# A refitted static schedule for windowed attention followed by an MLP mixer: zero-stride score mask, later masks, a new DMA model in the planner

## The chip, the cores and the metric

The kernel runs on one core of one Trainium2 chip. The metric is the device time in microseconds (us), of which the median of several executions is quoted. A profile gives the span of one execution, which is about 1.8 us shorter than the time measured for it. The engines are called as in the profile: PE (TensorE, matmuls), PEld (TensorE weight loads), DVE (VectorE), ACT (ScalarE), POOL (GpSimd) and SP (SyncE, here only an issuer of transfers).

## The reference, cut to what matters

```python
# attention: q, k, v are (4, 8, 768, 64) fp32
scores = (1/sqrt(64)) * q @ k^T
keep   = (key < 4) | ((0 <= query - key) & (query - key < 128))   # 4 sink keys + a window of 128
a      = softmax(where(keep, scores, -1e9)); x = a @ v            # -> x: (4, 768, 512)
# mixer
h  = relu(x^T @ w_tok1) @ w_tok2        # over the sequence, 768 -> 256 -> 768
u  = x + h^T
out = u + relu(u @ w_ch1) @ w_ch2       # over the channels, 512 -> 1536 -> 512
```

Only the blocks of the scores near the diagonal and the four sink keys are computed. Heads go in eight groups of four (groups 0 and 1 are batch 0, groups 4 and 5 batch 2, and so on).

## The kernel before

Every piece of work is a task with a duration, engines that may run it, and a priority. A planner simulates the engines and the transfers while the kernel is built. The order in which tasks start in that simulation is the order in which they are written to each engine, and that order is then fixed. Priorities are built from the stage and a table of corrections, `BIAS`, that was fitted.

```python
LOADS = "v0 v1 tok1 tok2 ch1a ch1b ch1c ch2a ch2b q2 k2 v2 q3 k3 v3".split()   # POOL's load queue
DMA_LAG = 1.2
LATE_LAG = 4.0
LATE_AT = 57
BIAS = {'ca2': 15, 'ut3': -0.6, 'tok11': -0.3, 'ca2.1': -8, ...}

        def drain(to):                    # the planner's model of the DMA
            ...
                heads = [x for x in queues.values() if x and x[0][1] <= drained + 1e-9]
                ...
                    step = min([step] + [x[0][2] * len(heads) for x in heads])
                    for x in heads:
                        x[0][2] -= step / len(heads)          # queues share equally
                ...
                        finish(x.pop(0)[0], drained + (LATE_LAG if drained > LATE_AT else DMA_LAG if drained > 14 else 1.0))
```

The lag is the time that the planner allows between the end of a transfer's share and its semaphore. It is 1.0 us up to a planned time of 14 us, then 1.2 us, and 4 us after 57 us. The masks of the early groups are added on PE (an additive mask, `mneg`, times the identity); later groups are multiplied by `mask0` or `mask1` after the exponential.

```python
    mneg = sb.tile([P, 2, 2, 2, P], BF16, name="mneg")       # every block stored twice
    ...
                        for i in range(2):
                            nc.tensor.matmul(bank(slot)[:, i, 0:w], ident,
                                             mneg[:, min(u, 1)].rearrange("p x c q -> p (x c q)")[:, 0:w],
                                             start=True, stop=False, skip_group_check=True)
    ...
    t_mask = add("DVE", 0.5, lambda t: nc.vector.memset(mask0, 1.0), prio=1)
    t_mask = add("POOL", 0.8, lambda t: build_mask(mask0), [t_mask], prio=1.5)
    ...
```

The softmax here doesn't subtract the row's maximum and nothing guards it: scores larger than these inputs give would overflow.

## Time and profile before

The time before was 207.21 us (206.95 to 207.47, three runs).

| what | value | view |
|---|---|---|
| PE busy | 198.4 of 205.6 us, 97% | page, part 1 |
| granted PE clock | 9 tenths or more in every slice; mean 0.999 | page, part 2; list of cores |
| chain that ended last | 85% PE | page, part 4 |
| first transpose / first channel matmul / last matmul start | 6.06 / 30.54 / 202.13 us | trace |

The page of the kernel before, cut: part 1 (busy time, share of the span and instructions of each engine), the rows of PE and of its granted clock in forty slices of the span, and part 4 (the chain that ended last, by engine).

```profile
PE 198.4 (97%) x1633; PEld 115.4 (56%) x1633; DVE 97.1 (47%) x230; ACT 109.5 (53%) x184; POOL 72.9 (35%) x123
PE   7889999999989999999999999999999999999993
PEclk9999999999999999999999999999999999999999
PE 85%; DMA 9%; DVE 3%; issue 1%; POOL 0%; SPq 0%; POOLq 0%; DVEq 0%
```

PE is full except in the first 15 us (slices 1 to 3), in slice 12 (about 60 us) and in the last slice. A busy PE need not stream at its best: the Trainium skill, Perfetto Trace Analysis, section Identifying the Most-Contended Engine, says that the busy share of matmuls is a poor measure of how near one is to the limit. So I used start times. Successive 512-column matmuls start 216 ns apart when nothing stands in the way, and a distance clearly longer is a stall. The first 11 matmuls, which only warm the engine, were 427 ns apart. The Trainium skill, TensorE: Matmul & The Clock Gate, section "Wait — 56ns, not 53.3ns?", gives 215.7 ns for the warm array and 426.7 for the cold one; this trace agrees with both.

The waits of PE in the kernel before (what PE wrote, and its line; what it waited for; us in total, times, longest):

```profile
PE ps_ga L1038 <- DVE warm L340: 1.3, 1, 1.3
PE ps_gb L789 <- DVE x_bb L816: 0.9, 1, 0.9
PE ps_sa L696 <- ACT kTa L334: 0.7, 1, 0.7
PE ps_ga L640 <- DVE qbb L336: 0.6, 1, 0.6
PE ps_gd L794 <- DMA vaa<-in_v_dram: 0.3, 1, 0.3
PE ps_gc L794 <- DVE pTb L725: 0.2, 1, 0.2
```

The wait for `warm` is the start of the program. All the others together are 2.7 us, little more than 1% of the time. With the first 6 us and the tail left aside, that is the budget of a better order. The 0.9 us for `x_bb` are the one at 60 us:

```profile
61.05 0.27 PE L789 MATMUL ps_gb<-vsink,pka 128*128 128x260 bf16 x1 [0.86 <-DVE x_bb L816]
```

(The timeline gives the start, the duration, engine, line, operation, and in brackets the idle time before and what ended it.)

### The profile page before, as it was taken

Reading aid. Unit: us, or ns where it says so; the run is one execution under the profiler, and the core shown is the slowest. Engines: PE = TensorE matmul, PEld = TensorE weight load, DVE = VectorE, ACT = ScalarE, POOL = GpSimd, SP = SyncE. Lnnn points to the kernel's source line nnn. Section 1 sums busy time; section 2 is a strip of 40 time slices with the busy share of each in tenths; the row PEclk is TensorE's granted clock in tenths of the full one; section 3 lists DMA queues with packets and bytes.
Section 4 is the critical chain, followed back from the end, with each engine's and each line's share of the span. In section 5 each row is a group of like instructions: output and inputs, shape, how many; then the busy total and the mean of one; then the engine's idle time right before and its main releaser. Section 6 shows DMA issues by size and latency. Waiting matters only on the chain.

```text
span 205.6 us, 4197 instructions
## 1 busy us (share of the span) xinstructions
PE 198.4 (97%) x1633; PEld 115.4 (56%) x1633; DVE 97.1 (47%) x230; ACT 109.5 (53%) x184; POOL 72.9 (35%) x123
## 2 busy tenths in 40 slices
PE   7889999999989999999999999999999999999993
PEld 2436776565557566665565544575565445655453
DVE  7679470166969948403284333862365222001122
ACT  2799667788866872178721306948612204753200
POOL 8918981016006799302997100204840000000000
PEclk9999999999999999999999999999999999999999
DMA  5999999999499959999969968620012442001122
GB/s 180 364 199 186 205 197 203 340 272 167 142 300 205 217 80 147 150 153 237 222 162 146 195 149 172 211 45 3 0 51 75 98 137 102 3 0 51 51 105 102
DMA packets 74869, 30.97 MB, mean 151 GB/s; under 512 B 63650, under 2 KB 71202, under 8 KB 74850
## 3 DMA queue, kind: packets, MB, share of 16 engines
q0 software_dynamic: 29680, 10.22, 41.5%
q1 hardware_dynamic: 43938, 18.85, 41.2%
q10 hardware_dynamic: 1232, 1.64, 2.3%
q8 instruction: 13, 0.21, 0.4%
q14 instruction: 6, 0.05, 0.1%
HBM read 26.77 MB, written 6.29 MB: 161 GB/s over the span
## 4 chain that ended last, share of the span: by engine, by line
PE 85%; DMA 9%; DVE 3%; issue 1%; POOL 0%; SPq 0%; POOLq 0%; DVEq 0%
PE ps_gd L938 9%; PE ps_ga L957 8%; PE ps_gb L938 8%; PE ps_ga L938 8%; PE ps_gb L957 7%; DMA vaa<-in_v_dram 7%; PE ps_gc L957 7%; PE ps_gd L957 6%; PE ps_gc L938 6%; DMA k32a<-in_k_dram 3%; PE ps_sb L696 3%; PE ps_sa L696 2%; PE ps_gc L860 2%; PE ps_ga L860 1%; PE ps_gb L860 1%; DVE pTa L734 1%
## 5 line engine op out<-in xcount | busy, mean ns | idle before, releaser
L938 PEld LDWEIGHTS <-w_ch 128*128 128x128 bf16 x384 | 36.8, 98 | 25.7 <-issue 0.6
L957 PEld LDWEIGHTS <-v 128*128 128x128 bf16 x312 | 28.3, 98 | 28.1 <-issue 1.4
L957 PE MATMUL ps_ga<-w_ch,v 128*128 128x512 bf16 (+1 forms) x96 | 23.4, 366 | 0.0
L919 ACT ACTIVATE v<-ps_ga 128x384 bf16<-128x384 f32 x20 | 9.8, 491 | 23.8 <-PE ps_ga L938 18.9
L957 PE MATMUL ps_gd<-w_ch,v 128*128 128x512 bf16 x72 | 18.5, 379 | 0.0
L957 PE MATMUL ps_gb<-w_ch,v 128*128 128x512 bf16 (+1 forms) x72 | 16.6, 352 | 0.0
L919 ACT ACTIVATE v<-ps_gd 128x384 bf16<-128x384 f32 x25 | 12.3, 491 | 8.0 <-PE ps_gd L938 7.6
L957 PE MATMUL ps_gc<-w_ch,v 128*128 128x512 bf16 (+1 forms) x72 | 16.4, 352 | 0.0
L919 ACT ACTIVATE v<-ps_gb 128x384 bf16<-128x384 f32 x21 | 10.3, 491 | 7.6 <-PE ps_gb L938 7.4
L938 PE MATMUL ps_gd<-uTa,w_ch 128*128 128x384 bf16 x60 | 12.2, 326 | 0.0
L725 POOL TENSOR_TENSOR pTc<-pTc,mask 128x512 bf16<-128x512 bf16 x3 | 3.5, 1151 | 23.1 <-ACT pTc L714 23.1
L336 POOL CAST kbb<-k32b 128x768 bf16<-128x768 f32 x6 | 5.4, 920 | 17.2 <-DMA k32b<-in_k_dram 17.2
L938 PE MATMUL ps_ga<-uTb,w_ch 128*128 128x384 bf16 x56 | 11.4, 326 | 0.0
L938 PE MATMUL ps_gd<-uTb,w_ch 128*128 128x384 bf16 x56 | 11.4, 326 | 0.0
L938 PE MATMUL ps_gb<-uTa,w_ch 128*128 128x384 bf16 x52 | 10.6, 326 | 0.0
L860 PEld LDWEIGHTS <-w_tok 128*128 128x128 bf16 x96 | 9.0, 98 | 2.4 <-issue 0.4
L379 POOL DMA_DIRECT2D vaa<-in_v_dram x4 | 6.0, 1493 | 12.0 <-PE ps_gc L798 11.1
L714 ACT ACTIVATE pTa<-ps_sb 128x1024 bf16<-128x1024 f32 (+1 forms) x7 | 6.5, 929 | 6.2 <-PE ps_sb L696 6.2
L938 PE MATMUL ps_gb<-uTb,w_ch 128*128 128x384 bf16 x44 | 9.0, 326 | 0.0
L336 POOL CAST qbb<-q32b 128x768 bf16<-128x768 f32 x7 | 6.1, 884 | 6.3 <-DMA q32b<-in_q_dram 6.3
L938 PE MATMUL ps_ga<-uTa,w_ch 128*128 128x384 bf16 x40 | 8.1, 326 | 0.0
L919 ACT ACTIVATE v<-ps_gc 128x384 bf16<-128x384 f32 x13 | 6.4, 491 | 2.8 <-PE ps_gc L938 2.5
(318 smaller groups left out, 435.5 us busy)
## 6 DMA issues: line engine op xcount, KB each, us to landing
q32a<-in_q_dram SPq DMA_DIRECT2D x4, 384.0 KB, 4.2
vaa<-in_v_dram POOLq DMA_DIRECT2D x4, 384.0 KB, 11.6
vab<-in_v_dram POOLq DMA_DIRECT2D x4, 384.0 KB, 10.9
w_ch<-in_moe_w_ch_dram POOLq DMA_DIRECT2D x3, 512.0 KB, 7.7
w_ch<-in_moe_w_ch_dram POOLq DMA_DIRECT2D x2, 768.0 KB, 12.0
out_dram<-oa SPq DMA_DIRECT2D x6, 256.0 KB, 2.0
q32b<-in_q_dram SPq DMA_DIRECT2D x8, 192.0 KB, 4.8
k32b<-in_k_dram SPq DMA_DIRECT2D x8, 192.0 KB, 5.1
```

What stands on the lines that cost most here:

```text
L336: on(t).tensor_copy(out=o, in_=i)
L379: t = add(eng, hold, lambda t: e.dma_start(out=o, in_=i), deps, prio=prio, dma=work)
L696: nc.tensor.matmul(bank(slot)[:, i, at:at + w].rearrange("p (c q) -> p c q", q=P), qkT(kT, g, j)[ds(64 * i, 64), kt], qkT(qT, g, j)[ds(64 ...
L714: nc.scalar.activation(dst[:, :, 512 * u:512 * u + w], bank(slot)[:, :, 0:w], AF.Exp, scale=scale)
L725: on(t).tensor_tensor(out=dst[:, :, 0:2 * P], in0=dst[:, :, 0:2 * P], in1=mask0.rearrange("p i c q -> p i (c q)"), op=ALU.mult)
L734: nc.vector.tensor_tensor(out=v3, in0=v3, in1=mask1.rearrange("p o c q -> p o (c q)").to_broadcast([P, full - lo, 2 * P]), op=ALU.mult)
L860: nc.tensor.matmul(flat(slot)[:, 0:GH * D], w_tok1[:, n, ts(tt, P)], x[:, n, ds(a * GH * D, GH * D)], start=(n == 0), stop=(n == NT - 1))
L919: nc.scalar.activation(o, i, AF.Relu)
L938: nc.tensor.matmul(flat(slot)[:, 0:HS], w_ch1[:, c, ts(ft, P)], uT_[:, c, ds(half * HS, HS)], start=(c == 0), stop=(c == NC - 1))
L957: nc.tensor.matmul(flat(slot)[:, 0:cw], v1[:, ft, ts(st, P)], w_ch2[:, ft, ds(c0, cw)], start=(ft == 0), stop=(ft == NF - 1 and b > 0), sk ...
```

## The change

The change does four things at once. The mask operand of the scores is stored once and its middle block is read twice with a zero stride. The multiplicative masks get a later priority. The planner shares the DMA engines by a weight for each transfer, `run`, that stands for its descriptor length, with new work figures and a lag of 2.0 instead of 1.2 us. And the priorities and the lists of allowed engines are fitted anew on that model.

```diff
-LOADS = "v0 v1 tok1 tok2 ch1a ...
+LOADS = "v0 v1 tok2 tok1 ch1a ...
+FIRST_TURNS = [[('ACT', 'DVE'), ('ACT', 'DVE')], ['DVE', 'DVE'], ['DVE', 'DVE'], ['DVE', 'DVE']]
-DMA_LAG = 1.2
+DMA_LAG = 2.0
 LATE_LAG = 4.0
 LATE_AT = 57
-BIAS = {'ca2': 15, 'ut3': -0.6, ...            # 34 entries
+BIAS = {'mask': 17.2, 'Lv1': 0.5, ...          # about twice as many
...
-                    step = min([step] + [x[0][2] * len(heads) for x in heads])
+                total = sum(x[0][0].run for x in heads)
+                    step = min([step] + [x[0][2] * total / x[0][0].run for x in heads])
...
-    mneg = sb.tile([P, 2, 2, 2, P], BF16, name="mneg")
+    mneg = sb.tile([P, 5, P], BF16, name="mneg")
...
+                            if u == 1:
+                                nc.tensor.matmul(o.rearrange("p (x w) -> p x w", x=2), ident,
+                                                 mneg[:, 2:4].rearrange("p (o c) q -> p o (c q)", o=1).to_broadcast([P, 2, 2 * P]),
...
-    load v:    work 0.63 * n
+    load v:    work 0.63 * n, run=0.21          # short descriptors get a small share
-    load tok2: work 2.2
+    load tok2: work 2.0, run=2.0
-    t_mask = add("DVE", 0.5, lambda t: nc.vector.memset(mask0, 1.0), prio=1)
+    t_mask = add("DVE", 0.5, lambda t: nc.vector.memset(mask0, 1.0), prio=1 + BIAS.get("mask", 0))
...                                              # also LATE_CAST, MASK_ENG; run= for the other transfers
```

The lines for the loads are shortened.

## The prediction

> **What bounds the kernel.** TensorE. The page gives PE 198.4 us of a 205.6 us span (97%), granted clock 0.999; the chain of waits is 85% PE. Start times of successive matmuls show PE at its streaming rate: 512 columns every 216 ns, 384 every 163 ns. At those rates the work from the first transpose (6.06 us) on would take about 193.5 us; it takes 196.2. So about 2.7 us are recoverable stalls. By the waits of PE and the gaps between starts: before the first scores 0.9 us (ACT's copy of kT); before group 1's transposes 0.6 (DVE casts qbb at 11.10, though its load landed at 9.53); before the first PV 0.35 (load of v, landed at 15.57); in 53 to 62 us 1.4 (DVE masks and normalisations). The first 6 us and the 3.4 us tail lie outside.
>
> **What the change removes, adds, moves.** PE does the same columns. The zero-stride operand streams; I expect 216 ns still. mneg shrinks from 1024 to 640 elements: DVE memset 0.48 to about 0.3 us, POOL selects 1.29 to about 0.9. The multiplicative masks (2.1 us on POOL, 1.2 on DVE) move later, so DVE casts kba about 0.4 us sooner and the token weights are issued sooner. The built order transposes k before q and copies kT on ACT beside qT on DVE; before, ACT did both, 2 x 0.7 us. POOL, not DVE, casts group 1's first q and k. The other transposed copies of groups 0 and 1 go to DVE, which frees about 2.5 us of ACT (nearly full from 8.9 to 20). The load queue becomes v0, tok2, tok1, v1: same bytes, so v1 lands near 21.7 instead of 18.5 us; its first PV comes near 22.5, still in time.
>
> **On the critical path.** v0 should land near 15.6 us as before: its small packets move at 15 KB/us while q and k load, at 150 KB/us after. The Trainium skill, DMA: Bandwidth & Descriptors, section Queues, rings and completion order, says each DMA engine alternates between queues by packet; this trace agrees. The gain is that about 0.9 us more independent PE work stands ahead of that wait. So start-up gives 0.8 to 1.2 us. In 44 to 62 us group 4's transposes stand earlier on PE, closer to loads that landed at 56.4 to 61.7 us: the x_bb stall should shrink, with 0.3 to 0.9 us of new waits for q or k; net +0.6 us. The remaining 140 us run at PE's rate.
>
> **Predicted:** 207.2 - 1.0 - 0.7 = about 205.5 us, range 204.2 to 206.9. Faster by over 2% (4.1 us, more than all stalls) 0.03; within 2% 0.94; slower by over 2% 0.03.
>
> **What would show it.** Waits of PE before 16 us: kT at 0.5 or less instead of 0.7, qbb's 0.6 gone, v0 still waited for, until 15.5 to 15.7. First ch1 matmuls near 29.6 instead of 30.5 us. Mask matmuls 216 ns. PE busy about 198 us. Tail 3.4 us.
>
> **What would make it wrong.** POOL casts slowed beside DVE (DVE casts took 1.3 us beside POOL's DMA issuing, 0.5 alone), so that group 1 waits for POOL; DVE, with four more 0.95 us copies, delaying normalisation; v1 later than its PV; new waits for loads of groups 3 to 5 near 50 to 75 us.

## The result, and the profile after

The changed kernel took 206.34 us (median of six, 205.86 to 209.39); the kernel before took 207.34 us. The ratio of the fast runs is 0.9952, 95% interval 0.9931 to 0.9972. Ratios here are the mean time of one kernel's fast runs over that of the other's fast runs of the same rounds, so they are not quite the ratio of the medians quoted. Executions over 1.5% slower than the fastest of the same kernel are left out of the means.

The execution that was profiled first was the 209.39 us one, with a granted clock of 0.992; it counts as slow and comes back below. For the comparison I ran the unchanged file again under a new label (`after_again`), whose profile is of a fast run (206.08 us, span 204.4). Its page and its waits of PE, the same views as above:

```profile
PE 196.5 (96%) x1616; PEld 115.1 (56%) x1633; DVE 95.0 (46%) x235; ACT 110.0 (54%) x188; POOL 65.4 (32%) x110
PE   7799999999989999999999999999999999999993
PE 75%; DMA 19%; DVE 1%; ACT 1%; issue 1%; SPq 1%; ACTq 0%; DVEq 0%
```

```profile
PE ps_ga L1049 <- DVE warm L347: 1.3, 1, 1.3
PE ps_gc L646 <- ACT ob L341: 0.8, 1, 0.8
PE ps_sa L707 <- DVE qTa L343: 0.6, 1, 0.6
PE ps_ga L646 <- POOL dm L366: 0.4, 1, 0.4
PE ps_gb L646 <- POOL kbb L343: 0.3, 1, 0.3
```

PE has 1616 matmuls in this record and 1633 in the other: 17 records are missing, and with them most of the difference of 1.9 us in its busy time. That busy time is no evidence of less work; the slow profile of the same file has all 1633 and 198.5 us. Of the waits before, `qbb` and the load of v are gone; `kTa` has become `qTa` and lost a little; `dm`, `kbb` and `ob` are new. (`dm` names the first transposes; DVE's cast of `kba`, which they read, ended at about the same time.) Without the start of the program the sum is 2.1 us here and 2.8 in after_c below, against 2.7 before. The DMA share of the chain, 19% instead of 9, is to about half one load of v, under way from 30.2 to 51.4 us; PE has no listed wait for it.

To see where the time came from I cut the start times of matmuls at the first channel matmul (the end of the start-up) and at the last matmul:

| us | first transpose | first scores | first PV | first channel matmul | from there to the last matmul | tail |
|---|---|---|---|---|---|---|
| before | 6.06 | 8.49 | 15.61 | 30.54 | 171.59 | 3.4 |
| after_again | 6.27 | 8.16 | 15.71 | 29.83 | 171.08 | 3.5 |
| after_c (a third profile of the same file) | 6.27 | 8.16 | 15.82 | 30.05 | 171.20 | 3.5 |

The spans differ by 1.2 and 0.9 us: 0.7 and 0.5 in the start-up, 0.5 and 0.4 in the rest. One profile of each kernel is not enough for tenths. Three profiles with the old start-up order (before, and the experiments zero_stride and masks_moved) give 30.54, 30.37 and 30.50 for the first channel matmul. Six with the new start-up order and the new model (the slow one, after_again, after_c, and three of the kernel called late54 below, which differs only near 60 us) give 30.14, 29.83, 30.05, 30.37, 29.95 and 30.13. The means are 30.47 and 30.08, so this landmark moved by 0.4 us. The rest is 171.85 us on the mean of the three old ones and 171.14 of the two fast new ones, 0.7 us less.

**Start-up.** PE's timeline in the kernel before, then in after_again with one line of DVE (lines left out):

```profile
6.06 0.82 PE L640 MATMUL ps_ga<-ident,qba 128*128 128x128 bf16 x6
8.49 0.39 PE L696 MATMUL ps_sa<-qTa,kTa 64*128 64x256 bf16 x4 [0.70 <-ACT kTa L334]
...
11.70 0.51 PE L640 MATMUL ps_ga<-ident,qbb 128*128 128x128 bf16 x6 [0.59 <-DVE qbb L336]
...
15.61 0.22 PE L794 MATMUL ps_gd<-vaa,pTa 128*128 128x65 bf16 x2 [0.31 <-DMA vaa<-in_v_dram]
```

```profile
5.45 0.76 DVE L343 CAST kba<-k32a 128x768 bf16<-128x768 f32 x1
6.27 0.51 PE L646 MATMUL ps_ga<-ident,kba 128*128 128x128 bf16 x6 [0.43 <-POOL dm L366]
...
8.16 0.40 PE L707 MATMUL ps_sa<-qTa,kTa 64*128 64x256 bf16 x4 [0.62 <-DVE qTa L343]
...
10.85 0.51 PE L646 MATMUL ps_ga<-ident,qbb 128*128 128x128 bf16 x6
11.62 0.51 PE L646 MATMUL ps_gb<-ident,kbb 128*128 128x128 bf16 x6 [0.26 <-POOL kbb L343]
...
15.71 0.23 PE L805 MATMUL ps_gb<-vaa,pTa 128*128 128x65 bf16 x2
```

Both steps that the prediction named happened: `qbb` comes without a wait, and the first PV no longer waits for v. But each gave its time to a neighbour. POOL casts `kbb` right behind `qbb`, and PE now stands for that. The first transposes begin at 6.27 instead of 6.06, because the new order takes k before q: the first load of k landed at 5.43 us and DVE's cast of it took 0.76, while q landed at 5.14 in the kernel before and ACT's cast of it was done at 6.01. Counted by start times against the streaming rate, the stalls from 7 to 16.5 us were:

| us | before | after_again | after_c |
|---|---|---|---|
| before the first scores | 0.87 | 0.78 | 0.78 |
| first transposes of q, group 1 | 0.63 | 0.10 | 0.10 |
| first transposes of k, group 1 (POOL's cast) | 0 | 0.42 | 0.42 |
| second cast of k, group 1 | 0 | 0 | 0.11 |
| first PV (load of v) | 0.35 | 0 | 0 |
| second transposed q of group 1 (DVE's copy), inside PV | 0 | 0.29 | 0.39 |
| sum | 1.85 | 1.59 | 1.80 |

So a gain of 0.9 us on two rows (0.53 and 0.35) came with a loss of 0.7 to 0.9 us on others. (The missing records of after_again leave two false gaps of 0.216 us, which I did not count.) Much of the 0.4 us in the landmark may be chance, too. In the profile of before the clock was still cold for the first transposes, which were 107 ns apart instead of 56, and the twelfth transpose started 0.24 us later than in after_again, although the first had started 0.21 us earlier. The trace's record of the granted clock has the full clock from 7.04, 6.62 and 6.80 us on in the three profiles with the old order, and from 4.35 to 5.40 in five of the six with the new one. The sixth, a profile of late54, got it at 6.65: its twelfth transpose came 0.16 us late, its first channel matmul (30.13) did not. How much of the 0.4 us is the order and how much the clock is therefore not shown.

**Near 60 us.** The wait for `x_bb` has become a wait of about the same size for the buffer `ob`. PE in after_again, then ACT:

```profile
58.88 0.50 PE L646 MATMUL ps_gb<-ident,qba 128*128 128x128 bf16 x6
60.18 0.49 PE L646 MATMUL ps_gc<-ident,qba 128*128 128x128 bf16 x6 [0.81 <-ACT ob L341]
```

```profile
56.86 0.84 ACT L341 ACTIVATE qba<-q32a 128x768 bf16<-128x768 f32 x1 [1.62 <-DMA q32a<-in_q_dram]
57.89 0.84 ACT L341 ACTIVATE qba<-q32a 128x768 bf16<-128x768 f32 x1 [0.19 <-DMA q32a<-in_q_dram]
58.64 1.00 ACT L725 ACTIVATE pTc<-ps_sb 128x1024 bf16<-128x1024 f32 x1
59.54 0.59 ACT L341 ACTIVATE ob<-ps_gc 128x512 f32<-128x512 f32 x1
```

The second transposes of q need the PSUM buffer `ps_gc`. It is held by an output tile of the first batch, which PE had finished by about 58.3 and ACT copies to `ob` only at 59.54. ACT had stood 1.62 us for a load of q, and once that had landed, two casts and an exponential stood ahead of the copy in its queue. The Trainium skill, TensorE: Matmul & The Clock Gate, in the specification table at its head, calls the queues of ScalarE and VectorE strict first-in first-out. The trace agrees: the load landed at 56.75, and nothing ran on ACT between 55.2 and 56.9 us.

The `x_bb` of the kernel before was a wait of the same kind on the other engine. There DVE stood 1.19 and 0.53 us for loads of q and k of group 4, which landed at 58.78 and 59.77, and the normalisation `x_bb` that frees PE's buffer came only at 60.57, behind their casts. So the new order moved this stall from DVE to ACT; what causes it, an engine held by a late load with other work behind it, stayed.

**The slow run.** In the profile of 207.7 us span, the same place was worse. Its waits of PE (the first line), its row of PE's clock, and four windows of 2 us (busy time and instructions of each engine, granted clock, DMA share, GB/s):

```profile
PE ps_gd L646 <- DVE x_bb L827: 2.0, 1, 2.0
PEclk9999999999996999999999999999999999999999
60.00:62.00 2.00, 0.49 (x6) 0.41 (x6) 1.63 (x3) 1.46 (x3) 1.99 (x3) 1.00 0.84 147
62.00:64.00 2.00, 1.42 (x14) 0.92 (x13) 1.94 (x4) 1.19 (x3) 0.96 (x3) 0.59 1.47 186
64.00:66.00 2.00, 2.00 (x12) 0.75 (x9) 0.88 (x3) 1.57 (x2) 1.22 (x3) 0.55 2.12 175
66.00:68.00 2.00, 2.00 (x19) 1.43 (x17) 1.29 (x2) 0.54 (x3) 1.42 (x4) 1.00 1.36 247
```

And DVE and PE in the same run (lines left out):

```profile
60.37 1.07 DVE L343 CAST kba<-k32a 128x768 bf16<-128x768 f32 x1 [2.04 <-DMA k32a<-in_k_dram]
62.10 0.42 DVE L827 TENSOR_TENSOR x_bb<-ps_gd,rca 128x256 bf16<-128x256 f32 x1
62.58 0.80 PE L646 MATMUL ps_gd<-ident,kba 128*128 128x128 bf16 x6 [1.99 <-DVE x_bb L827]
64.17 1.82 PE L968 MATMUL ps_gb<-w_ch,v 128*128 128x512 bf16 x4
```

The name in the list of waits is only the last link. The normalisation `x_bb` frees the buffer `ps_gd` that PE's transposes write. It stood on DVE behind a cast of k, and that cast waited for a load whose last semaphore step came at 60.25 us, 1.4 us later than in after_again (58.86), and then took 1.07 us instead of 0.56. The other 15 of the load's 16 steps were there by 58.98 (58.20 in after_again). The Trainium skill, DMA: Bandwidth & Descriptors, section "Why a DMA increments its semaphore by 16 and not by 1", says that the engines of one transfer finish independently; here one of them was 1.3 us behind. That is no mark of the slow run: in after_again the last step of the load of q that ACT stood for was 1.44 us behind the others (55.31 and 56.75). What differed is which load the late step struck, and how long PE stood for it. PE then stood twice, for 0.6 and 2.15 us, with six short transposes between. After that the granted clock was 0.59 and 0.55 in two stretches of 2 us (by the trace's record it was half from 62.38 to 65.79), and 512-column matmuls took 400 to 427 ns instead of 216. So one stall cost twice: first the wait, then about 1.6 us of slow matmuls (an estimate: half of the 3.2 us from 62.58 to 65.79). The section "What's actually happening" of the page on TensorE says that the clock is throttled after an idle window of about 3.4 us that runs freely. Here 2.7 us of idle within 3.1 us were enough.

In the three experiment calls the mean clock of each run is on record. Six of 33 runs of the kernel before (209.31 to 210.48 us) and one of 12 of the changed kernel (209.02) also had 0.992. No profile fell on those, so that they are the same event is likely, not shown. The record counts all but the 210.48 us one as fast, so they are inside the ratios of the experiments, and those of before make most of them smaller. With runs below a clock of 0.995 left out, the ratios to before are 0.9967 (after_again), 0.9942 (late54), 1.0001 (zero_stride), 1.0089 (masks_late), 0.9935 (late54_b), 0.9952 (sink_swap), 1.0014 (masks_moved), 1.0168 (old_model), 1.0031 (model_only, three runs), 0.9956 (after_c) and 0.9957 (late54_c).

### The profile page after: what moved, and what is told of

It is laid out like the page before. It is cut to its first block, busy times and chain, and to the rows that moved or that the text cites. A ratio compares the mean times of both kernels' runs of the same rounds, so it can differ in the third digit from the quotient of the medians.

```text
span 207.7 us, 4189 instructions
## 1 busy us (share of the span) xinstructions
PE 198.5 (96%) x1633; PEld 115.6 (56%) x1633; DVE 95.4 (46%) x235; ACT 110.4 (53%) x188; POOL 65.4 (32%) x110
## 4 chain that ended last, share of the span: by engine, by line
PE 82%; DMA 9%; DVE 4%; ACT 2%; issue 0%; SPq 0%; ACTq 0%; DVEq 0%
PE ps_ga L968 10%; PE ps_gd L949 8%; PE ps_gb L949 8%; PE ps_gc L949 8%; PE ps_gb L968 7%; DMA k32a<-in_k_dram 7%; PE ps_gc L968 6%; PE ps_ga L949 5%; PE ps_gd L968 5%; DMA vs_c<-in_v_dram 3%; PE ps_sb L707 3%; PE ps_ga L871 2%; PE ps_sa L707 2%; PE ps_gb L871 2%; PE ps_gd L913 1%; PE ps_gb L913 1%
## 5 line engine op out<-in xcount | busy, mean ns | idle before, releaser
L968 PE MATMUL ps_ga<-w_ch,v 128*128 128x512 bf16 (+1 forms) x108 | 25.8, 361 | 0.0
L930 ACT ACTIVATE v<-ps_gc 128x384 bf16<-128x384 f32 x22 | 10.8, 490 | 19.0 <-PE ps_gc L949 16.3
L968 PE MATMUL ps_gb<-w_ch,v 128*128 128x512 bf16 (+1 forms) x84 | 20.4, 367 | 0.0
L968 PE MATMUL ps_gd<-w_ch,v 128*128 128x512 bf16 x48 | 12.3, 379 | 0.0
L949 PE MATMUL ps_gb<-uTb,w_ch 128*128 128x384 bf16 x56 | 11.4, 326 | 0.0
L949 PE MATMUL ps_gc<-uTb,w_ch 128*128 128x384 bf16 x52 | 10.6, 326 | 0.0
L949 PE MATMUL ps_gc<-uTa,w_ch 128*128 128x384 bf16 x48 | 9.8, 326 | 0.0
L385 POOL DMA_DIRECT2D vab<-in_v_dram x4 | 5.8, 1440 | 8.9 <-PE ps_gc L809 4.8
L932 DVE TENSOR_SCALAR v<-ps_gd 128x384 bf16<-128x384 f32 x5 | 2.8, 556 | 11.8 <-PE ps_gd L949 11.8
L949 PE MATMUL ps_ga<-uTb,w_ch 128*128 128x384 bf16 x40 | 8.1, 326 | 0.0
## 6 DMA issues: line engine op xcount, KB each, us to landing
w_ch<-in_moe_w_ch_dram POOLq DMA_DIRECT2D x3, 512.0 KB, 10.5
```

The lines of the kernel that those rows point to most:

```text
L385: t = add(eng, hold, lambda t: e.dma_start(out=o, in_=i), deps, prio=prio, dma=work, run=run)
L930: nc.scalar.activation(o, i, AF.Relu)
L932: nc.vector.tensor_scalar(out=o, in0=i, scalar1=0.0, scalar2=None, op0=ALU.max)
L949: nc.tensor.matmul(flat(slot)[:, 0:HS], w_ch1[:, c, ts(ft, P)], uT_[:, c, ds(half * HS, HS)], start=(c == 0), stop=(c == NC - 1))
L968: nc.tensor.matmul(flat(slot)[:, 0:cw], v1[:, ft, ts(st, P)], w_ch2[:, ft, ds(c0, cw)], start=(ft == 0), stop=(ft == NF - 1 and b > 0), sk ...
```

## The experiments

All had five rounds. Every kernel gave a correct result.

### The file unchanged, for a fast profile: after_again

> The changed kernel itself, unedited: what is wanted is a profile of it in the fast state. Theory A (the group 4 k load is late): PE waits between 59 and 64 us of the span for 1.5 to 2.7 us in all, for a cast or an x_bb that stands behind the landing of k32a near 60 us; where that idle stretch is short enough the matmuls after it keep 216 ns per 512 columns and the run is fast, near 206.3; where it is long they fall to about 400 ns for a while, as in the profile at hand (209.4). Theory B (start-up gave less than expected and nothing else matters): the stall at 59 to 64 us is absent in a fast run, and the start-up gain is 0.4 us or less.

Measured: 206.53 us (206.08 to 207.53) against 207.39 of before, ratio 0.9955 [0.991, 0.9999]. The gain is there again, and its profile is the one shown above. The stall at 59 to 64 us was 0.8 us, shorter than the first theory said and not absent as the second one said.

### The zero stride alone: zero_stride

```diff
 kernel before, with
-    mneg = sb.tile([P, 2, 2, 2, P], BF16, name="mneg")
+    mneg = sb.tile([P, 5, P], BF16, name="mneg")
+    (selects, memset and mask matmuls as in the changed kernel; planner costs and order untouched)
```

> The kernel before with the score mask stored once and read with a zero stride, and nothing else (the planner keeps its old times, so the order stays). My theory: the mask matmuls stay at 216 ns, the time is within 0.3 us of before. Rival: a zero-stride moving operand streams slower; then the six 512-column mask matmuls of the middle score units take more than 216 ns and the first scores come later.

Measured: 207.47 us, ratio 0.9982 [0.9943, 1.0021]. The zero-stride matmuls start 226 or 227 ns apart, exactly as the contiguous ones in the same places before; the other 512-column mask matmuls keep 215 or 216. DVE's memset of `mneg` took 0.33 us and POOL's two selects 0.53 and 0.41, shorter than before (0.48, and 1.29 for both). Nothing waited for them. The zero stride is free and is worth nothing that can be seen.

### The later masks with the old priorities: masks_late

```diff
 kernel before, with
-BIAS = {'ca2': 15,
+BIAS = {'mask': 17.2, 'ca2': 15,
+    (the five mask tasks read BIAS.get("mask", 0) as in the changed kernel)
```

> The kernel before with only the priority of the multiplicative masks moved back (17.2), old planner and old priorities. My theory: casts and issues of the first 6 us move forward, yet PE's start is held by the landing of q and k (5.1 and 5.5 us) and by v0 (15.6 us), so 0 to 0.4 us are gained. Rival: the masks cost start-up a full microsecond, and 0.8 us or more are gained.

Measured: 209.38 us (208.81 to 211.16), ratio 1.0085 [1.0039, 1.0132]. Both theories expected a gain and were wrong. Its longest waits of PE, without the one for the start of the program:

```profile
PE ps_gd L789 <- DVE x_bb L816: 1.4, 1, 1.4
PE ps_gd L789 <- ACT pkb L771: 1.0, 1, 1.0
PE ps_gd L794 <- DMA vaa<-in_v_dram: 0.7, 1, 0.7
```

The first scores came at 8.04 instead of 8.49 us, but 0.37 of these 0.45 us are there at the twelfth transpose already: in this profile the full clock came at 4.95 us, before the first transpose, and not at 7.04. That the later masks made the start faster is not shown. The wait for v rose (0.7 instead of 0.3), and the new plan was worse near 60 us. One changed priority moves the whole schedule.

### Only the mask instructions moved, nothing replanned: masks_moved

```diff
 kernel before, after the order has been made:
+        late = [t for t in todo if t in mask_tasks]
+        todo = [t for t in todo if t not in mask_tasks]
+        at = todo.index(t_dm) + 1
+        todo[at:at] = late
```

> The kernel before, its plan kept, and only the seven instructions that build the multiplicative masks moved in the finished order, behind the build of dm. Theory: moving them costs nothing and is worth little, 206.9 to 207.4 us, so the 2 us that masks_late lost came from planning everything anew with old priorities, not from the move. Rival: late masks themselves cost, by POOL and DVE work landing in the busy 9 to 17 us stretch: 208 or more.

Measured: 207.88 us against 207.67, ratio 0.9994 [0.9943, 1.0044]. The wait for `qbb` rose to 0.9 us and the first scores stayed at 8.47. POOL builds the masks at 9.2 to 10.5 us here and at 8.5 to 10.1 in masks_late, so nearly at the same place. The move by itself is worth nothing that can be seen. So the 2 us that masks_late lost came from replanning, not from the masks.

### The new priorities on the old DMA model: old_model

```diff
 changed kernel, with
-DMA_LAG = 2.0
+DMA_LAG = 1.2
-    ... every run= weight and new work figure
+    ... the old work figures, equal shares
```

> The changed kernel with the planner's old DMA rule: equal shares among queues, old amounts of work, lag 1.2 us; the new priorities stay. Theory: the new priorities only make sense with the model that they were fitted to, so the order falls apart: 207.5 to 210 us, with waits of PE for v or for casts in the first 20 us or in 44 to 70 us. Rival: priorities alone carry the gain, and the time is 206.0 to 206.8.

Measured: 211.40 us (210.06 to 211.91), ratio 1.0147 [1.0092, 1.0202]. The loss is larger than the 207.5 to 210 us expected. The two longest waits of PE, without the one for the start of the program:

```profile
PE ps_sb L707 <- DVE kTa L343: 0.8, 1, 0.8
PE ps_sb L707 <- ACT pTc L725: 0.8, 1, 0.8
```

The first channel matmul came at 31.79 instead of about 30.1 us. The new priorities (with the new operand, lists and load order, which this run keeps) lose 3.7 us against the kernel before when the old model plans with them.

### The new DMA model with the old priorities: model_only

```diff
 kernel before, with
-DMA_LAG = 1.2
+DMA_LAG = 2.0
+    (the weighted sharing, all run= weights and work figures of the changed kernel)
```

> The kernel before with only the planner's new DMA model (sharing by descriptor length, the new works, lag 2.0 us); priorities, engine lists, load order and mask operand are the old ones. This is the missing cell of the two by two: old priorities with old model 207.4, new priorities with new model 206.5, new priorities with old model 211.4. Theory A (model and priorities are fitted to one another, neither has a value alone): slower than before by 0.5 to 4 us, 208 to 211.5. Rival B (the better model is itself the gain and the priorities only polish it): at most 206.8.

Measured: 209.78 us median, from 206.53 to 212.40. Three of six runs had a clock of 0.992 or 0.982 (210.45, 212.38, 212.40); the other three took 206.53, 208.34 and 209.10. By fast runs: 0.9994 [0.992, 1.0067]. The median fell in the range of the first theory, the fast runs do not decide, and the smallest time is even below the rival's limit. What can be said is that this kernel scatters over 6 us where the others scatter over 1 to 4. In its profile (209.10 us) the first channel matmul was at 32.53, two microseconds late, and the rest took 171.31 us. Its two largest waits of PE:

```profile
PE ps_gd L863 <- DVE x_ba L831: 1.7, 2, 1.4
PE ps_gc L643 <- DVE qba L339: 1.4, 1, 1.4
```

With the other three cells of this two by two (207.5, 211.4 and 206.3 us) it says that neither half has been seen to bring the gain alone.

### The lag threshold at 54: late54, late54_b, late54_c, with after_c

In the planner's own times, which are no measurements, the two loads of k of group 4 had landed at 58.0 and 62.6 us in the old plan and at 57.4 and 58.5 in the new one. In after_again they landed at 58.86 and 60.01. The second of them drains just before 57 in the new plan and so gets a lag of 2 us instead of 4. The plan then takes them for landed too early.

```diff
 changed kernel, with
-LATE_AT = 57
+LATE_AT = 54
```

About a dozen groups of PE instructions near 60 us change places: the scores of group 3 and token matmuls go ahead of transposes of k.

> One number of the planner: LATE_AT 57 becomes 54, so that it believes the loads of group 4's k land 4 us, not 2 us, after their last byte. The built order differs from the changed kernel's only in about twelve groups of matmuls near 60 us: the k transposes of group 4 stand behind the scores and the token matmuls. Theory A: the 1.5 to 2.7 us stall goes, the time is 204.0 to 205.2 us, and no run falls into the slow state. Theory B, or a stall that comes from DVE's own load: 206 or more, as before.

Measured: 206.09 us (205.66 to 207.14), ratio to before 0.9924 [0.9883, 0.9964], next to 0.9955 of after_again. By its time this is theory B (206 or more), not theory A.

> The kernel with LATE_AT 54 a second time, beside the next one on the same chip. Theory A (the change lost its middle gain to group 4's transposes, which the planner put too early): again 205.6 to 206.6 us, about 0.4 us under the changed kernel, no run near 209. If it comes out at the changed kernel's 206.3 to 206.5, the first result was scatter.

Measured: 206.34 us (205.44 to 206.97), ratio 0.9914 [0.9863, 0.9966]. That lies in the range of theory A and also in that for scatter, so it decides nothing.

> The changed kernel as it stands, for a comparison in one call with the next: 206.2 to 206.8, ratio to before 0.995 to 0.997, as in the two earlier sets of runs (0.9952, 0.9955).

> The changed kernel with the threshold at 54 instead of 57. Theory A (a dozen groups of PE instructions near 60 us, moved away from loads of k that the plan took for landed, are worth something): 0.3 to 0.5 us below the run before it, 205.9 to 206.3. Rival B (the two earlier ratios of 0.9924 and 0.9914 are scatter of the loads): within 0.2 us of it, either side.

Measured: after_c 206.29 us (205.94 to 209.02), ratio 0.9966 [0.9913, 1.0019]; late54_c 206.41 us (206.05 to 207.02), ratio 0.9946 [0.9909, 0.9984]. The medians are 0.12 us apart in the wrong direction, so the expected 0.3 to 0.5 us are not there. Over all, at a clock above 0.995, the mean is 206.49 us for 16 runs of the changed kernel and 206.33 for 18 of late54; a single run scatters by 0.5 us, so a difference of 0.16 is not shown. The profile of late54_c shows the mechanism, which did work:

```profile
59.61 0.34 PE L707 MATMUL ps_sb<-qTb,kTb 64*128 64x256 bf16 x4
60.10 0.51 PE L646 MATMUL ps_gc<-ident,qba 128*128 128x128 bf16 x6
60.63 1.02 PE L968 MATMUL ps_gd<-w_ch,v 128*128 128x512 bf16 x4
```

PE has scores and channel matmuls where it had stood, and runs through. In this profile a wait for a transposed load came later instead (at 120.5 us, 0.8 us for `kTa`, where after_again and after_c have none), and in late54_b three small waits stayed between 59.8 and 61.6 us (0.35, 0.34 and 0.19). None of the 18 runs had the clock of 0.992, against two of 18 of the changed kernel; that is too few to call it a cure.

### One instruction of the start-up moved: sink_swap

In the changed kernel DVE stands 0.4 to 0.7 us for the load `vs_c` with the second cast of `kbb` behind it. I moved the sink cast that needs this load behind that cast, in late54.

```diff
 late54, after the order has been made:
+        todo.remove(sink)
+        todo.insert(todo.index(kbb) + 1, sink)
```

> LATE_AT 54, and in the order handed to the engines one instruction pair of DVE moved: the cast of the sink values stands after the last cast of kbb, not before it. Nothing is planned anew. In the profiles DVE stood 0.7 us on the landing of vs_c with that kbb cast behind it, and PE waited 0.2 to 0.6 us for it and for the qTb copy after it. Theory C (start-up gave less than predicted because DVE is held in order behind vs_c): the kbb cast starts near 13.6 instead of 14.96 us, PE's waits for kbb and qTb go, the first ch1 matmuls come 0.4 to 0.9 us earlier and the time falls by as much, to 205.2 to 205.7. Rival: start-up is set by ACT's exponentials or by v0, and the time stays within 0.2 us of the run beside it.

Measured: 206.61 us (206.14 to 207.17), ratio 0.9937 [0.9884, 0.9989]. The waits for `kbb`'s second cast and for `qTb` are gone, and the first channel matmul came at 29.76 us, the earliest of all. The theory named the waits rightly, but its time did not come: it is 0.3 us above that of late54_b (206.34), a little outside what the rival allowed, too. A gain of 0.2 us in the start-up (29.76 against 29.95) is under the scatter of the runs.

## Why the prediction was right or wrong

The prediction was 205.5 us with a range of 204.2 to 206.9, and "within 2%" with 0.94. The medians measured were 206.34, 206.53 and 206.29. The range holds them and so does the class. The size was too large: 1.7 us were expected and about 1.0 came (means of 207.47 in 27 runs and 206.49 in 16 at a clock above 0.995; the 95% interval of the difference, worked out from these runs, is 0.7 to 1.3). By steps:

- **PE bounds the kernel and at most 2.7 us can be had.** It held: no version came under 205.4 us in a single run, and 207.2 less 2.7 is 204.5.
- **The zero-stride operand still streams at 216 ns.** Right in substance: 226 or 227 ns in most pairs and 215 in one of after_c, never longer than the contiguous operand in the same place, and zero_stride shows that it is worth nothing by itself.
- **Start-up 0.8 to 1.2 us.** This is the step that failed, by its size. The landmark moved by 0.4 us on the mean of several profiles (30.08 instead of the 29.6 expected, from 30.47). The prediction counted the waits that would go and did not count those that the same moves would make: POOL's cast of `kbb` (0.42 us), DVE's copy of `qTb` (0.29 to 0.39) and the first transposes 0.2 us later, by the order of k before q that it named itself. Of the 0.4 us, a part may be the clock's chance described above, so the true gain can be smaller still. It had listed "POOL casts slowed beside DVE" and DVE's additional copies among what could go wrong, but without a charge in the sum.
- **v0 is still waited for, until 15.5 to 15.7.** Wrong. It landed at 15.13 to 15.27 in the new order, and the first PV at 15.71 waited for nothing. More work ahead of a wait only helps until that work is itself what is late.
- **kT at 0.5 or less, qbb's 0.6 gone.** The first wait became one for `qTa`, 0.6; the second went. Half right.
- **v1 near 21.7 and in time.** It landed 0.9 us later than that, at 22.57 and 22.54 in the two fast profiles, and its first PV started at 22.76 and 22.98. It was in time, with 0.2 to 0.4 us to spare.
- **44 to 62 us: net gain 0.6, with 0.3 to 0.9 of new waits for loads of q or k.** The `x_bb` stall went, but a new stall of 0.8 to 0.9 us, for a PSUM buffer that ACT had not emptied because it had stood for a load of q, took its place. The prediction put the old stall down to DVE's masks and normalisations; the trace of before has DVE standing 1.19 and 0.53 us for loads ahead of them. The part after the first channel matmul gained 0.7 us on the mean of few profiles (0.5 against the profile of before alone). The term was near; the reason given was only partly the one seen, and much of the gain is spread over tenths that I cannot assign.
- **Tail 3.4 us, PE busy about 198.** The tail was 3.5. PE's busy time was 198.5 us in the profile with all records.

Where the gain lies is then answered only in part. Not in the operand (zero_stride), not in the place of the mask instructions (masks_moved), not in the new priorities without the model (old_model); model_only did not show it either. By elimination it lies in priorities, engine lists, load order and model fitted together, but as the fast runs of model_only are undecided, this is argued and not shown. How the 0.7 us in the long part split among single waits stays open.

## What to carry to other kernels

When a kernel is at 97% of its busiest engine, add up the recoverable stalls first: they are the ceiling. An order that removes one wait can hand it to the next feeder in line (here 0.9 us of waits went and 0.7 to 0.9 came), so charge new waits in the same sum. Ask of each wait which load stands at its root: moving it to another engine does not remove it. Priorities fitted on a model of the machine belong to that model: here the new ones lost 3.7 us on the old model. And look at the slowest profile as well as at a typical one: here 2.7 us of stall on PE were followed by half the clock.

## What the Trainium skill lacked or had wrong

- TensorE: Matmul & The Clock Gate, section "What's actually happening", gives one idle window of about 3.4 us for the throttle. Here PE idled 0.6 and 2.15 us within 3.1 us, with six transposes between, and the clock was then 0.59 and 0.55 in two stretches of 2 us. So no single wait of 3.4 us was needed; the clock was halved at 62.38, 2.0 us after the last of the six transposes began.
- DMA: Bandwidth & Descriptors, section "Why a DMA increments its semaphore by 16 and not by 1", says that the engines finish independently but gives no spread. One load of k had 15 of 16 steps at 58.98 and the last at 60.25 us, 1.3 us later; in the fast after_again a load of q had its last step 1.4 us after the others.
- Advanced Engine Details and Errata, section VectorE Performance Modes, notes that GPSIMD and the two-port modes of VectorE block each other and gives no size there (the page on SBUF has sizes for other instructions). The same DVE cast (128x768, fp32 to bf16) took 0.56 us when POOL was idle (before, at 59.89) and 1.07 us beside POOL's DMA issue and selects (the slow run), but also 0.56 us beside a DMA issue (zero_stride, at 7.05). What decides it is not shown here.
- No page that I read has the cost of a zero stride in the moving operand of a matmul: 226 or 227 ns from one 512-column matmul of a pair to the next, the same as without it (zero_stride and before), and 215 in one pair of after_c.
